# Decoding weight blocks throughout attention, three w_out blocks ahead of the MLP, and softplus as one unit

## The chip, the cores and the metric

The kernel runs on one core of a Trainium2 chip. The metric is the device time of one execution in microseconds (us), the median of several runs. A profile of one further execution tells where the time goes; its span runs from the first to the last recorded instruction.

## The reference

Three stages follow each other; all results are float32.

```
# 1. Nystrom attention, batch 4, heads 8, sequence 576, head size 64, 32 landmarks
A  = softmax(q  @ k_lm.T / 8)      # q_lm, k_lm: means over 18 neighbouring rows
Bm = softmax(q_lm @ k_lm.T / 8)
C  = softmax(q_lm @ k.T / 8)
Z  = Bm.T / (norm1(Bm) * norminf(Bm) + 1e-6);  six times: Z = 2*Z - Z @ Bm @ Z
x  = (A @ Z @ C @ v)               # then (2304 tokens, 512)
# 2. dense MLP, d_ff 2048
h  = x @ w_in;   g = max(h, 0) + log1p(exp(-abs(h)));   x = g @ w_out
# 3. top-1 mixture of 8 experts: token -> argmax(x @ w_gate)
out = gate_prob * sigmoid(x @ w_output_gate)[e] * (relu(x @ w1[e]) @ w2[e])
```

w_in and w_out come as 64-bit floats. The kernel takes them as pairs of 32-bit integers, decodes each block to float32, and splits every matrix operand into a rounded high part and the rest (hi and lo), so that one product is three matmuls: hi*hi, hi*lo and lo*hi.

## The kernel before

**Attention** works on eight groups (a batch and half of its heads). The string PLAN lists its steps: K and V load a group, T transposes it, M makes landmarks, C and A are the two large softmaxes, N the Newton iteration of a batch, E and F the products that end in a batch's x, stored to a DRAM tensor xT_d. W decodes a block of 128 columns of w_in, O a block of 128 rows of w_out, X prepares the first 256 tokens of x. PLAN gives priorities; a planner makes each engine's final order from them, and may bring an instruction forward when its inputs are there and its buffer is free. Attention's q, k and v tiles have three buffers each, and the W, O and X loads use those same buffers from SP's queue. One decode (`decode_f64`, L87) is an Abs on ScalarE (L96) and three integer operations on VectorE (L97, L99, L101); then ScalarE copies the hi part (L106) and GpSimd, in attention, subtracts for the lo part (L107). Ten W blocks (NWA) and one O block are made there.

**The MLP** runs after it in an order written out by hand. Its unit of work is a pair: `gemm1` (L611) makes 256 columns of h for 256 tokens with 24 matmuls, softplus turns them into g, and `gemm2` (L650) adds g's product with two w_out blocks into accumulators with 12 matmuls, two pairs later (LAG). There are 9 chunks of 256 tokens with 8 pairs each; the first three chunks (JOINT) are interleaved, 24 turns, so that each weight block that is decoded serves three chunks. Meanwhile the 21 blocks that attention did not make are loaded by SP (`load_w`, L562) and decoded by VectorE and ScalarE (`weights`, L572), a generator of four units a block. 12 units, three blocks, are taken before the first turn (L876), three and five in the first two turns, and then four a turn, put among the parts of softplus: `softplus_a`, `softplus_b` and `softplus_c` stand at three places of the turn, and the last two belong to the pair before. SP also loads the gate weights (L845) before the second w_out block, and VectorE makes five small tables (L846 to L850) before the loop.

Gating and routing of the tokens are hidden in the later pairs. **The experts** follow, with tiles of 128 tokens; `t_h` (L967) transposes the hidden tile and splits it into hh and hlo, which have three buffers.

Of the kernel before, what the change touches and what calls it, by code (L numbers as in the profile page):

```python
# [1 line left out]

# [27 lines left out]
CH = 256  # L30
# [17 lines left out]
U = 1, 1, 2  # L48
# [38 lines left out]
def decode_f64(nc, pool, src, shape, tag="dect", **kw):  # L87

    w = src.rearrange("p a (n two) -> p a n two", two=2)
    lo32, hi32 = w[:, :, :, 0], w[:, :, :, 1]
    t = pool.tile(shape, I32, tag=tag, name="dect", **kw)
    a = pool.tile(shape, F32, tag="deca", name="deca", **kw)
    nc.scalar.activation(a, hi32.bitcast(F32), AF.Abs, scale=2.0 ** -112)  # L96
    nc.vector.tensor_scalar(t, a.bitcast(I32), 3, None, ALU.logical_shift_left)  # L97
    yield
    nc.vector.scalar_tensor_tensor(t, hi32, -0x80000000, t, ALU.bitwise_and, ALU.bitwise_or)  # L99
    yield  # L100
    nc.vector.scalar_tensor_tensor(a.bitcast(I32), lo32, 29, t, ALU.logical_shift_right, ALU.bitwise_or)  # L101
    yield a
# [13 lines left out]
def moe_nystrom_kernel(ctx: ExitStack, tc: tile.TileContext, q, k, v, w_in, w_out, w_gate, w_ogate, w1, w2,  # L116
# [23 lines left out]
    wo0 = [x0_pool.tile([128, DM], F32R, name=n) for n in ("wo0h", "wo0l")]  # L140


    with ExitStack() as actx:
# [241 lines left out]
        def decode_w_in(i):  # L385
            n = FF // 16
            raw = ld.tile([128, NC6 * 4 * D], I32, tag="kqv"[i % 3], name="raw")
            raw = raw[:, :8 * n].rearrange("p (k f) -> p k f", k=4)
            nc.sync.dma_start(raw, w_in.bitcast(I32).rearrange("(k p) f -> p k f", p=128)[:, :, 2 * n * i:2 * n * (i + 1)])
            a = list(decode_f64(nc, a3, raw, [128, 4, n], bufs=2))[-1]  # L390
            split_hi_lo(nc, a, whi[0][:, :, i * n:(i + 1) * n], wlo[0][:, :, i * n:(i + 1) * n], nc.gpsimd)
# [14 lines left out]
        def prep_x0():  # L406
            xr = ld.tile([128, 4, CH], F32, tag="k", name="x0r")
            nc.sync.dma_start(xr, xT_d[0].rearrange("(k p) n -> p k n", p=128)[:, :, :CH])
            split_hi_lo(nc, xr, x0[0], x0[1], nc.gpsimd)

        def prep_wo0():
            raw = ld.tile([128, 2 * DM], I32, tag="q", name="raw")
            nc.sync.dma_start(raw, w_out.bitcast(I32)[:128, :])
            a = list(decode_f64(nc, a3, raw.unsqueeze(1), [128, 1, DM], bufs=2))[-1]
            split_hi_lo(nc, a[:, 0], wo0[0], wo0[1], nc.gpsimd)
# [12 lines left out]
            "O": lambda _: prep_wo0(),  # L428
# [115 lines left out]
    with ExitStack() as mctx:  # L544
# [27 lines left out]
        def weights():  # L572

            for n, (kind, f) in enumerate(jobs):
                for a in decode_f64(nc, m2, raws.pop(n).unsqueeze(1), [128, 1, DM], tag="x2t"):
                    if a is None:
                        yield
                load_w(n + 3)
                yield
                a = a[:, 0]  # L580
                if kind == "o":
                    split_hi_lo(nc, a, woh[f], wol[f], nc.vector)
                else:
                    split_hi_lo(nc, a.rearrange("p (k f) -> p k f", k=4), wcols(whi, f), wcols(wlo, f), nc.vector)
                yield
# [38 lines left out]
        def softplus_a(h):  # L624
            t = sp.tile([128, 2, CH], F32, tag="t", name="t")
            u = sp.tile([128, 2, CH], F32, tag="u", name="u")
            l = sp.tile([128, 2, CH], F32, tag="l", name="l")
            nc.scalar.activation(t, h, AF.Abs)  # L628
            nc.scalar.activation(t, t, AF.Exp, scale=-1.0)  # L629
            nc.scalar.activation(u, t, AF.Identity, bias=1.0)  # L630
            yield
            nc.scalar.activation(l, t, AF.Ln, bias=1.0)  # L632
            nc.vector.scalar_tensor_tensor(u, u, -1.0, t, ALU.add, ALU.subtract)  # L633
            yield h, u, l

        def softplus_b(h, u, l):

            d = sp.tile([128, 2, CH], F32, tag="d", name="d")
            nc.vector.scalar_tensor_tensor(d, h, 0.0, u, ALU.max, ALU.subtract)  # L639
            nc.vector.tensor_tensor(l, l, d, ALU.add)  # L640
            return l

        def softplus_c(l):
            gh = m3.tile([128, 2, CH], F32R, tag="gh", name="gh")
            gl = m3.tile([128, 2, CH], F32R, tag="gl", name="gl")
# [194 lines left out]
        with tc.manual_schedule():  # L840
# [3 lines left out]
            for nm, src in ((0, w_gate), (1, w_ogate)):  # L844
                nc.sync.dma_start(wg[:, :, nm * NE:(nm + 1) * NE], src.rearrange("(k p) e -> p k e", p=128))  # L845
            nc.vector.tensor_copy(tri_b, cc("tri"))  # L846
            nc.vector.tensor_copy(one_b, cc("ones"))
            nc.vector.memset(osum[:, 0], 0.0)
            nc.vector.tensor_copy(sgn[:, 0], cc("iota")[:1, :NE])
            nc.vector.tensor_scalar(sgn[:, 1], cc("iota")[:1, :NE], -1.0, None, ALU.mult)  # L850
            ga, gs, accs = {}, {}, {}
# [24 lines left out]
            units(12)  # L876
            for i in range(len(order) + LAG):
# [11 lines left out]
                u = ((0, 0, 3), (0, 2, 3))[i] if i < 2 else U  # L889
                if i - 1 in ga:  # L890
                    gs[i - 1] = softplus_b(*ga.pop(i - 1))
                if i < len(order):
# [6 lines left out]
                    units(u[0])  # L899
                    sp_ = softplus_a(h)  # L900
                    next(sp_)
                    if i - 1 in gs:
                        gs[i - 1] = softplus_c(gs[i - 1])
                    ga[i] = next(sp_)
                    units(u[1])
# [4 lines left out]
                if i - 1 in gs and i >= len(order):  # L910
                    gs[i - 1] = softplus_c(gs[i - 1])
                units(u[2])
# [20 lines left out]
    with ExitStack() as ectx:  # L933
# [10 lines left out]

        todo = iter(TAIL)
# [21 lines left out]
        def t_h(hs):  # L967
# [3 lines left out]
            hh = e3.tile([128, 4, 128], F32R, tag="hh", name="hh")  # L971
            hlo = e3.tile([128, 4, 128], F32R, tag="hlo", name="hlo")
# [114 lines left out]
```

## Time and profile before

| | us |
|---|---|
| median of 3 runs (lowest, highest) | 920.24 (918.68, 920.66) |
| the profiled execution's own time | 920.92 |
| its span | 919.1 |
| TensorE busy, share of the span | 863.8, 94% |
| VectorE busy | 660.8, 72% |
| ScalarE busy | 589.2, 64% |
| GpSimd busy | 209.6, 23% |

The profile names TensorE's matmuls PE and its weight loads PEld, VectorE DVE, ScalarE ACT, GpSimd POOL and SyncE SP; an engine's name with a q is its queue of DMA issues. "out<-in" names the tile written and the tiles read, L99 is a line of the kernel, and "xN" after it is a count. An idle time in square brackets stands before the instruction and names what ended it. Attention lies at 0 to 149.3 us of the span, the interleaved pairs at 149.7 to some 290 us, the other pairs reach to 610 us, and the experts to the end.

### The profile page before, as it was taken

Reading aid. Unit: us, or ns where it says so; the run is one execution under the profiler, and the core shown is the slowest. Engines: PE = TensorE matmul, PEld = TensorE weight load, DVE = VectorE, ACT = ScalarE, POOL = GpSimd, SP = SyncE. Lnnn points to the kernel's source line nnn. Section 1 sums busy time; section 2 is a strip of 40 time slices with the busy share of each in tenths; the row PEclk is TensorE's granted clock in tenths of the full one; section 3 lists DMA queues with packets and bytes.
Section 4 is the critical chain, followed back from the end, with each engine's and each line's share of the span. In section 5 each row is a group of like instructions: output and inputs, shape, how many; then the busy total and the mean of one; then the engine's idle time right before and its main releaser. Section 6 shows DMA issues by size and latency. Waiting matters only on the chain.

```text
span 919.1 us, 15441 instructions
## 1 busy us (share of the span) xinstructions
PE 863.8 (94%) x5826; PEld 717.5 (78%) x5826; DVE 660.8 (72%) x1121; ACT 589.2 (64%) x958; POOL 209.6 (23%) x109
## 2 busy tenths in 40 slices
PE   6998987599999999999999999998999999999996
PEld 3665655478788899999999998886878888888885
DVE  0846697787775546665546464668899999999994
ACT  2554564666666655555555555464888888888893
POOL 0001132000000000000000000024666677666662
PEclk9999997799999999999999999999999999999998
DMA  9856466323210000100111000141117459531600
GB/s 228 188 137 182 146 189 194 94 89 92 82 46 13 24 1 24 46 22 4 46 46 47 1 24 1 47 184 47 44 37 264 174 182 378 184 126 34 225 31 33
DMA packets 49516, 90.93 MB, mean 99 GB/s; under 512 B 5471, under 2 KB 32095, under 8 KB 47392
## 3 DMA queue, kind: packets, MB, share of 16 engines
q1 hardware_dynamic: 41408, 74.43, 26.1%
q0 software_dynamic: 3680, 10.78, 3.6%
q10 hardware_dynamic: 4352, 4.72, 1.5%
q8 instruction: 47, 0.77, 0.4%
q14 instruction: 29, 0.24, 0.1%
HBM read 134.46 MB, written 15.48 MB: 163 GB/s over the span
## 4 chain that ended last, share of the span: by engine, by line
PE 68%; DVE 13%; ACT 10%; issue 4%; DMA 4%; POOL 0%; SPq 0%; POOLq 0%; ACTq 0%; DVEq 0%
PE ps_h L618 16%; PE acc L657 14%; PE ps_g L956 12%; PE ps_y L982 11%; DVE dect L99 2%; DVE deca L101 2%; PE ps_hT L970 2%; PE ps_lg L682 2%; ACT t L629 2%; ACT u L630 2%; ACT deca L96 2%; ACT gh L646 1%; DVE u L633 1%; PE ps_t L184 1%; PE ps_t L160 1%
## 5 line engine op out<-in xcount | busy, mean ns | idle before, releaser
L478 DVE TENSOR_TENSOR lo<-raw,hi 128x1024 fp32r<-128x1024 f32 x129 | 228.7, 1799 | 8.8 <-ACT hi L476 8.6
L476 ACT ACTIVATE hi<-raw 128x1024 fp32r<-128x1024 f32 x176 | 176.8, 1063 | 8.4 <-DMA raw<-in_moe_w 8.3
L618 PE MATMUL ps_h<-xh,whi 128*128 128x256 f32 x512 | 147.4, 288 | 5.8 <-DVE d L639 4.1
L618 PE MATMUL ps_h<-xl,whi 128*128 128x256 f32 x512 | 144.9, 283 | 0.3 <-DVE xl L107 0.3
L618 PE MATMUL ps_h<-xh,wlo 128*128 128x256 f32 x512 | 144.8, 283 | 0.0
L647 DVE TENSOR_TENSOR gl<-l,gh 128x512 fp32r<-128x512 f32 x72 | 49.9, 692 | 129.0 <-ACT gh L646 129.0
L485 POOL DMA_INDIRECT xg<-x_d,gidx x23 | 37.8, 1645 | 452.4 <-ACT t L628 441.4
L478 POOL TENSOR_TENSOR lo<-raw,hi 128x1024 fp32r<-128x1024 f32 x47 | 115.9, 2468 | 35.3 <-ACT hi L476 35.2
L618 PEld LDWEIGHTS ps_h<-xh,whi 128*128 128x128 f32 x512 | 98.0, 191 | 11.4 <-DVE d L639 7.9
L618 PEld LDWEIGHTS ps_h<-xl,whi 128*128 128x128 f32 x512 | 98.0, 191 | 1.9 <-DVE xl L107 0.5
L618 PEld LDWEIGHTS ps_h<-xh,wlo 128*128 128x128 f32 x512 | 97.9, 191 | 0.0
L657 PE MATMUL acc<-woh,gh 128*128 128x512 f32 x240 | 96.2, 401 | 0.0
L657 PE MATMUL acc<-wol,gh 128*128 128x512 f32 x240 | 94.5, 394 | 0.0
L657 PE MATMUL acc<-woh,gl 128*128 128x512 f32 x240 | 94.3, 393 | 0.0
L628 ACT ACTIVATE t<-ps_h 128x512 f32<-128x512 f32 x72 | 42.6, 592 | 69.6 <-PE ps_h L618 50.0
L632 ACT ACTIVATE l<-t 128x512 f32<-128x512 f32 x72 | 45.5, 632 | 55.1 <-DVE gl L647 55.1
L982 PE MATMUL ps_y<-hi,hh 128*128 128x512 f32 x184 | 76.7, 417 | 0.2 <-ACT hh L974 0.2
L982 PE MATMUL ps_y<-hi,hlo 128*128 128x512 f32 x184 | 73.3, 398 | 1.7 <-DVE hlo L975 1.6
L956 PE MATMUL ps_g<-hi,x0l 128*128 128x512 f32 x184 | 73.9, 402 | 0.1
L982 PE MATMUL ps_y<-lo,hh 128*128 128x512 f32 x184 | 72.7, 395 | 0.0
L956 PE MATMUL ps_g<-hi,x0h 128*128 128x512 f32 x184 | 72.0, 391 | 0.0
L956 PE MATMUL ps_g<-lo,x0h 128*128 128x512 f32 x184 | 71.9, 391 | 0.0
(263 smaller groups left out, 1790.4 us busy)
## 6 DMA issues: line engine op xcount, KB each, us to landing
raw<-in_moe_w SPq DMA_DIRECT2D x88, 1024.0 KB
raw<-in_moe_w_in SPq DMA_DIRECT2D x16, 512.0 KB
raw<-in_moe_w_out SPq DMA_DIRECT2D x16, 512.0 KB
x_d<-x SPq DMA_DIRECT2D x9, 514.0 KB
k<-in_k SPq DMA_DIRECT2D x8, 576.0 KB
q<-in_q SPq DMA_DIRECT2D x8, 576.0 KB
v<-in_v SPq DMA_DIRECT2D x8, 576.0 KB
xT_d<-xo ACTq DMA_DIRECT2D x16, 288.0 KB
```

Source lines behind the costliest of these rows:

```text
L96: nc.scalar.activation(a, hi32.bitcast(F32), AF.Abs, scale=2.0 ** -112)
L99: nc.vector.scalar_tensor_tensor(t, hi32, -0x80000000, t, ALU.bitwise_and, ALU.bitwise_or)
L476: nc.scalar.activation(w[0][:, us], raw[i][:, us], AF.Copy)
L478: eng.tensor_tensor(w[1][:, us], raw[i][:, us], w[0][:, us].bitcast(F32), ALU.subtract)
L485: nc.gpsimd.indirect_dma_start(out=xg, out_offset=None, in_=src, in_offset=bass.IndirectOffsetOnAxis(ap=gidx[:, s:s + 1], axis=0))
L618: nc.tensor.matmul(ps[:, i], a[:, kk], b_[:, kk], start=n == 0, stop=n == 11)
L628: nc.scalar.activation(t, h, AF.Abs)
L632: nc.scalar.activation(l, t, AF.Ln, bias=1.0)
L647: nc.vector.tensor_tensor(gl, l, gh.bitcast(F32), ALU.subtract)
L657: nc.tensor.matmul(acc[tt], a[:, i, ts_], b_[f], start=f == 0 and n == 0, stop=f == NFF - 1 and n == 2)
L956: nc.tensor.matmul(ps, a[:, kk], b_[:, kk], start=n == 0, stop=n == 11)
L982: nc.tensor.matmul(y, a[:, kk], b_[:, kk], start=half == 0 and n == 0, stop=half == 1 and n == 11)
```

## The change

The decoding steps get buffers of their own (tag raw, two buffers) and their loads are issued from GpSimd's queue. Attention makes eight W blocks and three O blocks instead of ten and one; they are spread over PLAN, from after E1 on. The MLP takes no units before the loop. One softplus function does the whole of a pair's softplus in its own turn and takes three units at fixed places, none in turn 0; `EXTRA` adds one unit in turn 0 and three more in turns 5 and 8. A block's decode is begun with the split of the block before it. The number of blocks decoded in the loop is 21 as before. The gate's loads and the small tables move from before the loop to turn 2. The pools psm and pss change places in PSUM, and hh and hlo of the experts lie in the w_out tiles that attention filled.

```diff
-K1 T0 M0 M1 A0 C0 T1 K2 M2 C1 K3 V0 A1 K4 V1 T2 E0 C2 E1 T3 M3 N0 V2 K5 K6 V3 T4 A2 C3 A3 F0 V4 E2 M4 A4 M5 T5 K7 E3
-N1 X0 V5 M6 C4 T6 C5 C6 E4 M7 V6 V7 N2 A5 E5 W0 F1 N3 W1 W2 E6 W3 T7 A6 W4 O0 C7 A7 W5 F2 W6 E7 W7 F3 W8 W9
+K1 T0 M0 M1 A0 C0 T1 K2 M2 C1 K3 V0 A1 K4 V1 T2 E0 C2 E1 W0 T3 M3 N0 W1 V2 K5 K6 V3 T4 W2 A2 C3 A3 F0 W3 V4 E2 M4 A4
+W4 M5 T5 K7 E3 W5 N1 X0 V5 M6 C4 W6 T6 C5 C6 E4 M7 V6 V7 N2 A5 W7 E5 F1 N3 O0 E6 T7 A6 C7 A7 O1 F2 E7 O2 F3
-NWA = 10
+NWA = 8
+NWO = 3
+EXTRA = 0, 5, 8
...
     nc.scalar.activation(a, hi32.bitcast(F32), AF.Abs, scale=2.0 ** -112)
+    yield
     nc.vector.tensor_scalar(t, a.bitcast(I32), 3, None, ALU.logical_shift_left)
-    yield
     nc.vector.scalar_tensor_tensor(t, hi32, -0x80000000, t, ALU.bitwise_and, ALU.bitwise_or)
-    yield
     nc.vector.scalar_tensor_tensor(a.bitcast(I32), lo32, 29, t, ALU.logical_shift_right, ALU.bitwise_or)
     yield a
...
+        psm = actx.enter_context(tc.tile_pool(name="psm", bufs=1, space=PSUM))
         pss = actx.enter_context(tc.tile_pool(name="pss", bufs=2, space=PSUM))
-        psm = actx.enter_context(tc.tile_pool(name="psm", bufs=1, space=PSUM))
...
-            raw = ld.tile([128, NC6 * 4 * D], I32, tag="kqv"[i % 3], name="raw")
-            raw = raw[:, :8 * n].rearrange("p (k f) -> p k f", k=4)
-            nc.sync.dma_start(raw, w_in.bitcast(I32)...)
+            raw = ld.tile([128, 8 * n], I32, tag="raw", name="raw", bufs=2).rearrange("p (k f) -> p k f", k=4)
+            nc.gpsimd.dma_start(raw, w_in.bitcast(I32)...)
...
-        def prep_wo0():
-            raw = ld.tile([128, 2 * DM], I32, tag="q", name="raw")
-            nc.sync.dma_start(raw, w_out.bitcast(I32)[:128, :])
+        def prep_wo(f):
+            raw = ld.tile([128, 2 * DM], I32, tag="raw", name="raw", bufs=2)
+            nc.gpsimd.dma_start(raw, w_out.bitcast(I32)[f * 128:(f + 1) * 128, :])
...
         def weights():
+            dec = {}
+            def start(n):
+                if n < len(jobs):
+                    dec[n] = decode_f64(nc, m2, raws.pop(n).unsqueeze(1), [128, 1, DM], tag="x2t")
+                    next(dec[n])
+            def finish(n):
+                if n < len(jobs):
+                    dec[n] = next(dec[n])[:, 0]
+                    load_w(n + 3)
+            start(0)
+            finish(0)
+            yield
             for n, (kind, f) in enumerate(jobs):
...
+                nc.scalar.activation(hi, a, AF.Copy)
+                start(n + 1)
                 yield
+                nc.vector.tensor_tensor(lo, a, hi.bitcast(F32), ALU.subtract)
+                yield
+                finish(n + 1)
                 yield
...
+        def softplus(h, units):
...
             nc.scalar.activation(t, h, AF.Abs)
             nc.scalar.activation(t, t, AF.Exp, scale=-1.0)
             nc.scalar.activation(u, t, AF.Identity, bias=1.0)
             nc.scalar.activation(l, t, AF.Ln, bias=1.0)
+            units(1)
             nc.vector.scalar_tensor_tensor(u, u, -1.0, t, ALU.add, ALU.subtract)
             nc.vector.scalar_tensor_tensor(d, h, 0.0, u, ALU.max, ALU.subtract)
             nc.vector.tensor_tensor(l, l, d, ALU.add)
             nc.scalar.activation(gh, l, AF.Copy)
+            units(1)
             nc.vector.tensor_tensor(gl, l, gh.bitcast(F32), ALU.subtract)
+            units(1)
             return gh, gl
...
-            units(12)
             for i in range(len(order) + LAG):
...
                     h = gemm1(p, xs[c], *HB.get(i, ()))
...
+                    gs[i] = softplus(h, units if i else int)
+                    if i in EXTRA:
+                        units(1 if i == 0 else 3)
+                    if i == 2:
+                        nc.vector.tensor_copy(tri_b, cc("tri"))
...
+        hht = cycle([[wo0[j][f].rearrange("p (k n) -> p k n", k=4) for j in range(2)] for f in range(NWO)])
...
-            hh = e3.tile([128, 4, 128], F32R, tag="hh", name="hh")
-            hlo = e3.tile([128, 4, 128], F32R, tag="hlo", name="hlo")
+            hh, hlo = next(hht)
```

## Rows read from the trace of the kernel before

**Rows 1.** The page: busy time by engine, then TensorE and DMA in 40 slices.
```profile
PE 863.8 (94%) x5826; PEld 717.5 (78%) x5826; DVE 660.8 (72%) x1121; ACT 589.2 (64%) x958; POOL 209.6 (23%) x109
...
PE   6998987599999999999999999998999999999996
...
DMA  9856466323210000100111000141117459531600
```
**Rows 2.** Windows: from:to, length, busy us (instructions) by engine, TensorE clock, DMA share, GB/s.
```profile
9.84:149.67 139.83, 126.45 (x1580) 81.22 (x1580) 95.64 (x267) 75.79 (x171) 16.95 (x12) 0.97 0.68 178
5.00:35.00 30.00, 23.89 (x293) 15.97 (x294) 12.70 (x41) 11.94 (x31) 0.00 (x0) 1.00 1.10 247
120.00:149.67 29.67, 22.89 (x186) 12.38 (x185) 28.35 (x59) 18.76 (x38) 10.11 (x8) 0.88 0.60 182
149.67:176.63 26.96, 15.59 (x85) 14.18 (x86) 17.83 (x29) 13.71 (x24) 0.24 (x1) 0.69 0.44 141
176.63:277.31 100.68, 94.86 (x578) 80.81 (x576) 79.67 (x131) 66.42 (x114) 0.00 (x0) 1.00 0.25 76
```
**Rows 3.** TensorE in order of time: start, duration, line, tiles, count, idle before.
```profile
9.84 1.19 PE L184 MATMUL ps_t<-cst,k 96*128 96x96 f32 x6 [6.48 <-DMA cst<-in_consts]
...
92.71 0.69 PE L204 MATMUL ps_lm<-lmc,l 128*64 128x64 f32 x16 [2.94 <-ACT l L200]
...
147.97 1.33 PE L377 MATMUL ps_x<-at,wbd 64*128 64x288 f32 x4
149.67 0.58 PE L618 MATMUL ps_h<-x0h,whi 128*128 128x256 f32 x1 [0.37 <-ACT xo L379]
...
171.34 0.79 PE L657 MATMUL acc<-wo0h,gh 128*128 128x512 f32 x1 [11.37 <-ACT gh L646]
...
176.63 0.35 PE L618 MATMUL ps_h<-xh,whi 128*128 128x256 f32 x1
```
**Rows 4.** The chain that ended last, in order of time: start, duration, what.
```profile
151.56 6.49 DMA raw<-in_moe_w_out
...
280.45 2.75 PE acc L657 x12
283.20 2.87 PE ps_h L618 x24
```
**Rows 5.** VectorE and ScalarE in one turn of the interleaved pairs.
```profile
186.16 0.68 DVE L633 SCALAR_TENSOR_TENSOR u<-u,t 128x512 f32<-128x512 f32 x1
186.76 0.69 DVE L99 SCALAR_TENSOR_TENSOR dect<-raw,dect 128x512 int32<-128x512 int32 x1
187.48 0.69 DVE L101 SCALAR_TENSOR_TENSOR deca<-raw,dect 128x512 int32<-128x512 int32 x1
...
189.32 0.58 ACT L628 ACTIVATE t<-ps_h 128x512 f32<-128x512 f32 x1
...
191.13 0.62 ACT L646 ACTIVATE gh<-l 128x512 fp32r<-128x512 f32 x1
```
**Rows 6.** VectorE in order of time: two A steps, each first and last instruction.
```profile
42.68 0.78 DVE L320 STREAM_TRANSPOSE asm<-ps_a 128x576 f32<-128x576 f32 x1 [0.71 <-PE ps_a L218]
...
48.02 0.78 DVE L331 STREAM_TRANSPOSE at<-asm 128x576 f32<-128x576 f32 x1
...
132.33 0.71 DVE L320 STREAM_TRANSPOSE asm<-ps_a 128x576 f32<-128x576 f32 x1
...
145.34 0.77 DVE L331 STREAM_TRANSPOSE at<-asm 128x576 f32<-128x576 f32 x1
```
**Rows 7.** VectorE's groups at 120 to 149.67 us: line, shapes, count, busy, mean ns.
```profile
L99 DVE SCALAR_TENSOR_TENSOR dect<-raw,dect 128x512 int32<-128x512 int32 x7 | 7.0, 1005 | 0.0
...
L97 DVE TENSOR_SCALAR dect<-deca 128x512 int32<-128x512 int32 x7 | 3.5, 498 | 0.8 <-ACT deca L96 0.8
```
**Rows 8.** SP's issues: start, time until the last is issued, line, tiles, count.
```profile
5.26 6.84 SPq L173 DMA_DIRECT2D v<-in_v  x3
```
**Rows 9.** ScalarE in order of time: a decode that waits for its load.
```profile
91.16 1.22 ACT L96 ACTIVATE deca<-raw 128x512 f32<-128x512 f32 x2 [3.05 <-DMA raw<-in_moe_w_in]
```

More of the change, by code (lines that the diff above doesn't have):

```diff
@@ L1 @@
 from contextlib import ExitStack, nullcontext
+from itertools import cycle
 import numpy as np
@@ L47 @@
 LEAD = 1
-U = 1, 1, 2
 LAG = 2
@@ L139, in moe_nystrom_kernel @@
     x0 = [x0_pool.tile([128, 4, CH], F32R, name=n) for n in ("x0h", "x0l")]
-    wo0 = [x0_pool.tile([128, DM], F32R, name=n) for n in ("wo0h", "wo0l")]
+    wo0 = [[x0_pool.tile([128, DM], F32R, name=f"{n}{f}") for f in range(NWO)] for n in ("woh", "wol")]
     with ExitStack() as actx:
@@ L427, in moe_nystrom_kernel @@
             "X": lambda _: prep_x0(),
-            "O": lambda _: prep_wo0(),
+            "O": prep_wo,
             "W": decode_w_in,
@@ L553, in moe_nystrom_kernel @@
         pa = pool("pa", 1, space=PSUM)
-        woh = [wo0[0]] + [wo.tile([128, DM], F32R, name=f"woh{f}") for f in range(1, NFF)]
-        wol = [wo0[1]] + [wo.tile([128, DM], F32R, name=f"wol{f}") for f in range(1, NFF)]
-        due = [(3 * (f // 2) + 2 * (f == 1), "o", f) for f in range(1, NFF)]
+        woh = wo0[0] + [wo.tile([128, DM], F32R, name=f"woh{f}") for f in range(NWO, NFF)]
+        wol = wo0[1] + [wo.tile([128, DM], F32R, name=f"wol{f}") for f in range(NWO, NFF)]
+        due = [(3 * (f // 2) + 2 * (f == 1), "o", f) for f in range(NWO, NFF)]
         due += [(3 * (f // 2) - 2, "i", f) for f in range(NWA, NFF)]
@@ L572, in weights @@
         def weights():
-            for n, (kind, f) in enumerate(jobs):
[L575 to L578, printed above, removed]
-                yield
[L580 to L584, printed above, removed]
+            dec = {}
[10 more added lines that the diff above has]
+            yield
+            for n, (kind, f) in enumerate(jobs):
+                if kind == "o":
+                    a, hi, lo = dec.pop(n), woh[f], wol[f]
+                else:
+                    a, hi, lo = dec.pop(n).rearrange("p (k f) -> p k f", k=4), wcols(whi, f), wcols(wlo, f)
+                nc.scalar.activation(hi, a, AF.Copy)
+                start(n + 1)
+                yield
+                nc.vector.tensor_tensor(lo, a, hi.bitcast(F32), ALU.subtract)
+                yield
+                finish(n + 1)
                 yield
@@ L843, in moe_nystrom_kernel @@
             load_w(0)
[L844 to L851, printed above, removed]
+            gs, accs = {}, {}
             side = iter(())
@@ L898, in moe_nystrom_kernel @@
                         next(side, None)
[L899 to L905, printed above, removed]
+                    gs[i] = softplus(h, units if i else int)
[3 more added lines that the diff above has]
+                        nc.vector.tensor_copy(tri_b, cc("tri"))
+                        nc.vector.tensor_copy(one_b, cc("ones"))
+                        nc.vector.memset(osum[:, 0], 0.0)
+                        nc.vector.tensor_copy(sgn[:, 0], cc("iota")[:1, :NE])
+                        nc.vector.tensor_scalar(sgn[:, 1], cc("iota")[:1, :NE], -1.0, None, ALU.mult)
+                        for nm, src in ((0, w_gate), (1, w_ogate)):
+                            nc.sync.dma_start(wg[:, :, nm * NE:(nm + 1) * NE], src.rearrange("(k p) e -> p k e", p=128))
                     if i == nj - 1:
@@ L909, in moe_nystrom_kernel @@
                         xs[c + 1] = split_x(load_xr(c + 1))
-                if i - 1 in gs and i >= len(order):
-                    gs[i - 1] = softplus_c(gs[i - 1])
-                units(u[2])
                 if i >= len(order):
```

23 lines of the change are left out of this document (7 added, 16 removed).

## The prediction

> **What bounds the kernel now.** I read the page first: TensorE is busy for 94% of the span, so time can only come from where it idles or runs slowly, and the slices show that at the front, in the first, fifth to eighth and last of 40 [rows 1]. The windows then split that front into stages [rows 2]. In attention TensorE is busy 126.45 of 139.83 us at a mean clock of 0.97; VectorE is loose on the whole (95.64 us) but full at its end, 28.35 of 29.67 us. From the first MLP matmul to the fourth pair, 26.96 us, TensorE works 15.59 us at a clock of 0.69. In the interleaved turns after that it works 94.86 of 100.68 us. TensorE's order of time tells what the middle window waits for [rows 3]: attention's last matmul ends at 147.97 + 1.33 = 149.30 us, the first gemm1 starts at 149.67, and after three of them the first gemm2 idles 11.37 us for ScalarE's gh. The chain of waits shows what stands ahead of that gh, a 6.49 us load of a w_out block, and also what a pair costs where TensorE alone is the limit: 2.87 us for 24 matmuls of gemm1 and 2.75 us for 12 of gemm2, 5.62 us [rows 4]. After turn 18 this is the pace, and nothing of the change touches it.
>
> **The change part by part.** The sum is made against the profiled execution, 920.92 us (span 919.1 and 1.82 around it), 0.68 us above the median shown.
>
> *The wait before the first gemm2.* 12 units, three whole blocks, stand ahead of the first softplus and go; the w_out blocks 0 to 2 come from attention, so gemm2 of the first two pairs lacks none but block 3, which is decoded in turns 0 and 1. What is late next is the first softplus itself. Its chain by the distances of the same operations in a turn [rows 5]: from t to the fourth ScalarE operation 191.13 - 189.32 = 1.81 us; u ends some 0.1 us after that, then three VectorE operations in a row at 0.72 us each (187.48 - 186.76), a gh of 0.62, a gl of 0.69: 5.5 us. Two more gemm1 take 2 x 2.87 = 5.74 us meanwhile, so the stall goes to about nothing; that cover is gone if the splitting of x, which sits ahead on both engines, ends over 0.2 us late. So 11.37 us go. The 12 matmuls of the first gemm2 took 176.63 - 171.34 = 5.29 us after this idle time; at full pace 2.75, so 2.54 more go. The first three gemm1 took 171.34 - 11.37 - 149.67 = 10.30 us instead of 8.61, because TensorE was on its low clock after the thin end of attention; that 1.69 us I leave in. Sum -13.9 us; ends -15.6 (those too) and -10.9 (a stall of 3 us for a late gl).
>
> *The interleaved turns.* 16 turns (3 to 18) take 100.68 us [rows 2], 6.29 each against 5.62: 10.8 us are lost, and neither VectorE (79.67) nor ScalarE (66.42) is full, so it is their waiting for each other in the written order. The new order of one turn on VectorE, with 0.60 us between independent and 0.72 between dependent operations [rows 5]: u, d, l at 0.72, 0.72, then gh on ScalarE (0.7) and gl 1.4 us after l starts, with lo in between; 0.6 for gl, 0.45, 0.72 and 0.6 for the three decode operations: 5.2 us. ScalarE has t, exp, u, ln, hi, the next Abs and gh, and is free for the next t 4.7 us after this one. Behind gh, which waits for l, stands the next pair's t, and that has till 5.62. So the turn fits under TensorE, with 0.39 us to spare. The turns 5 and 8 take a second block, whose hi, lo and three decode operations follow each other in some 3.3 us. Two of them, 6.6 us, less 0.39 x 8 and a start margin of 0.3, leave a stall of about 3.2 us. So -10.8 + 3.2 = -7.6; ends -10.8 (lag hides both) and -4 (every turn 0.22 longer as well). The later pairs use the same softplus without units: 2.76 us of VectorE in 5.62, hidden.
>
> *Attention, its end.* The last A step runs on VectorE from 132.33 to 146.11 us, and an early one from 42.68 to 48.80, 6.1 us against 13.8 [rows 6]. Between its operations stand seven decodes, whose three operations are 7.0, 4.7 and 3.5 us [rows 7]. With those gone earlier, up to 7.7 us go from the end, since the last ps_x wait for that step.
>
> *Attention, its start.* The planner issues loads when a buffer is free, not where PLAN has them: SP issues V0, V1 and V2 by 12 us [rows 8]. GpSimd's queue is empty, so I expect W0 and W1, 1.05 MB, in the first microseconds, beside the loads on which the first transpose waits until 9.84 us [rows 3]. In that stretch the DMA engines are full, 247 GB/s [rows 2], so the two blocks push back the rest by 1.05/0.247 = 4.25 us at most, by nothing if SP's queue is served first. I take the 4.25, as full engines leave no spare. The Trainium skill, DMA: Bandwidth & Descriptors, section SWDGE vs HWDGE vs iDMA, says that loads from GpSimd and from SP lie in different queues of each DMA engine, which serves them in turn. By it the early blocks do get their share and the sum has the 4.25, without it 0; no row here shows both queues in that stretch.
>
> *Attention, loads that come late.* One decode waits 3.05 us for its block on ScalarE [rows 9], with the copies of another group behind it, and TensorE idles 2.94 us [rows 3]. I keep one such wait. With 11 early blocks in full DMA queues there may be more: the bound is 11 x 2.94 = 32 us, the other end is none. I take the row nearest, one as before, since SP's loads no longer share buffers with the blocks. GpSimd's 11 lo operations stay, and its issues stand between them. The Trainium skill, SBUF — State Buffer, section SBUF: two separate sides, speaks against the move: while VectorE holds the port that it shares with GpSimd, GpSimd can't write the descriptors of its loads. Here L99 takes 1.005 us beside GpSimd's subtractions [rows 7] against 0.69 in a turn [rows 5], so the two do meet; by that rule a load could lose an operation like L97, 0.5 us, and all 11 would be 5.5 us, most of it hidden by the second buffer.
>
> Attention: -7.7 + 4.25 = -3.5 us. Its floor: all idle time, 139.83 - 126.45 = 13.4, and 3% of clock, 4.2, go: -17.6.
>
> Sum: -3.5 - 13.9 - 7.6 = -25.0, 895.9 us in the profiled run, about 895 as a median.
>
> **Rivals.**
> 1. *Blocks land late and stretch attention.* Four loads of the kind of [rows 9] in the full stretch: 4 x 2.94 - 3.5 = +8.3 us in attention, total -13.2: 907. For it: the planner doesn't know how full the queues are. Against: after 40 us they are far from full [rows 1].
> 2. *Attention becomes as dense as TensorE allows*: -17.6 + 4.25 = -13.4, total -34.9: 886. For it: its VectorE has 44 us free. Against: Newton and A steps are chains.
> 3. *x comes late.* If the tiles of x lie where attention's last tiles were, their load starts at its end: 6.49 and some 1.6 us of splitting, against 3.3 until the second gemm1, +4.8: 900. Against: nothing of their pool changes.
> 4. *The decodes don't spread*, because GpSimd's queue holds loads behind lo operations that wait for ScalarE: no change in attention, 899.
> 5. *Slower: the fused softplus doesn't fit a turn.* ScalarE's gh waits for VectorE's l in the same turn and holds up hi, the next Abs and the next t. It turns the total to a loss when a turn passes 6.29 + 17.4/16 = 7.4 us; at 7.6 it is 16 x 1.31 = +21, total 924. For it: the turn today takes 6.29 with both engines a fifth idle. Against: the 5.2 us above, from measured distances.
>
> **How the numbers follow.** Forecast 0.46, rivals 0.22, 0.14, 0.07, 0.05 and 0.06. The time is the forecast's, 895. The range 883 to 910 takes in rivals 1 to 4 for the most part; outside lie rival 5 and the far tails of 1 and 2, together under 0.2. A measurement of this kernel can't tell less than 0.2%, 1.8 us, from no change. Slower 0.07: rival 5 and the far end of rival 1's 32 us. Same 0.03, faster 0.90.
>
> **What would show it.** In the trace after: no idle time of over 2 us before the first gemm2, and its 12 matmuls near 2.75 us; 16 turns in 90 to 94 us, with TensorE idle only near turns 6 and 9; two block loads on GpSimd's queue before 5 us and the first transpose near 14 us; the last A step in 6 to 8 us and attention's end near 146. I am wrong if ScalarE's Abs waits for raw again and again, if the first transpose isn't later, or if a turn stays at 6.2 us.

## The result, and the profile after

The changed kernel takes 925.01 us (median of 5 runs, 924.38 to 925.52) against 919.72 for the kernel before beside it: 1.0058 times, 95% interval 1.0044 to 1.0071. It is slower by 0.6%, and the forecast of 895 is wrong in sign. The page of the profile after hardly differs in TensorE's busy time [rows 1], while the span is 4.1 us longer, so on balance the loss is idle time. In the slices TensorE is thinnest in the first two, and its granted clock dips in the second, fifth and eighth.

```profile
PE 863.9 (94%) x5826; PEld 722.4 (78%) x5826; DVE 662.5 (72%) x1121; ACT 586.3 (64%) x958; POOL 218.8 (24%) x121
...
PE   4698899889998999999999998998999999999996
...
PEclk9899899999999999999999999999999999999999
DMA  9947424433210000100111000141107459531600
```

Both traces are cut at the same four instructions (gemm1 of turn 3, gemm1 of turn 19, a gemm1 at the end of the pairs, the last instruction), so that each row can be set beside a term of the forecast's sum.

| stretch | before | after | difference | forecast |
|---|---|---|---|---|
| to turn 3 | 176.63 | 172.40 | -4.2 | -3.5 - 13.9 = -17.4 |
| turns 3 to 18 | 100.68 | 97.05 | -3.6 | -7.6 |
| pairs after that | 321.27 | 332.20 | +10.9 | 0 |
| the rest, mostly experts | 320.52 | 321.55 | +1.0 | 0 |
| span | 919.1 | 923.2 | +4.1 | -25.0 |

The windows that give these lengths follow: first two of the kernel before that [rows 2] does not have, then those of the kernel after, the last two with the slow clock that two places below speak of. After the length stand busy us (instructions) of TensorE, its weight loads, VectorE, ScalarE and GpSimd, then TensorE's granted clock, the DMA share and GB/s.

```profile
277.31:598.58 321.27, 317.18 (x2097) 288.50 (x2098) 176.56 (x424) 182.50 (x322) 2.07 (x2) 1.00 0.08 25
598.58:919.10 320.52, 307.84 (x1486) 252.33 (x1484) 290.56 (x273) 249.51 (x327) 190.11 (x91) 0.99 0.39 139
```

```profile
163.70:172.40 8.70, 6.26 (x37) 5.22 (x38) 5.84 (x11) 6.87 (x13) 0.00 (x0) 1.00 0.71 216
172.40:269.45 97.05, 92.18 (x578) 83.30 (x576) 89.25 (x148) 71.25 (x123) 0.00 (x0) 0.98 0.32 99
269.45:601.65 332.20, 322.01 (x2098) 292.35 (x2097) 185.71 (x429) 181.85 (x324) 2.00 (x2) 0.98 0.08 25
601.65:923.20 321.55, 308.13 (x1486) 252.27 (x1484) 283.27 (x272) 249.01 (x326) 191.23 (x91) 0.99 0.39 139
40.00:45.00 5.00, 2.88 (x22) 1.95 (x22) 3.48 (x10) 2.80 (x7) 0.00 (x0) 0.50 0.65 179
444.00:449.00 5.00, 5.00 (x19) 4.04 (x19) 2.94 (x5) 2.33 (x4) 0.00 (x0) 0.66 0.00 0
```

TensorE in order of time (start, duration, line, tiles, idle before) says how the first stretch lost what it had won. The 11.37 us before the first gemm2 [rows 3] are 1.44, near the nothing that was forecast. But the first transpose is 3.2 us later than before, and two idle times of 5.63 and 3.58 us are new; attention's last matmul, ps_x, ends at 163.70 instead of 149.30. (Two of the MLP's first three gemm1, 5.74 us at full pace, now run ahead of it, so not all of these 14.4 us are lost.)

```profile
13.00 1.20 PE L185 MATMUL ps_t<-cst,k 96*128 96x96 f32 x6 [9.64 <-DMA cst<-in_consts]
...
42.12 0.59 PE L161 MATMUL ps_c<-dense 128*128 128x512 bf16 x1 [5.63 <-ACT ec L310]
...
93.29 0.59 PE L161 MATMUL ps_t<-dense 128*128 128x512 bf16 x1 [3.58 <-ACT lm L208]
...
162.94 0.76 PE L378 MATMUL ps_x<-at,wbd 64*128 64x288 f32 x4
164.69 0.38 PE L634 MATMUL ps_h<-xh,whi 128*128 128x256 f32 x1 [1.00 <-ACT xo L380]
...
169.27 0.50 PE L669 MATMUL acc<-woh,gh 128*128 128x512 f32 x1 [1.44 <-ACT gh L656]
```

ScalarE in the same stretch shows what stands behind them: the Abs of the first two blocks that it finds late, and the copy of x0r.

```profile
9.92 0.66 ACT L98 ACTIVATE deca<-raw 128x512 f32<-128x512 f32 x1 [7.89 <-DMA raw<-in_moe_w_in]
...
40.69 0.66 ACT L98 ACTIVATE deca<-raw 128x512 f32<-128x512 f32 x1 [6.17 <-DMA raw<-in_moe_w_in]
...
91.91 1.06 ACT L107 ACTIVATE x0h<-x0r 128x1024 fp32r<-128x1024 f32 x1 [6.50 <-DMA x0r<-xT_d]
```

and GpSimd's issues say why the one at 40.69 is late: two loads go at 1.31, but the fifth, which needs the buffer of the third, goes only at 30.19, after that one's decode, and arrives 10.5 us later.

```profile
1.31 1.73 POOL L389 DMA_DIRECT2D raw<-in_moe_w_in  x2 [0.86 <-POOLq L1076]
13.04 0.75 POOL L389 DMA_DIRECT2D raw<-in_moe_w_in  x1 [9.99 <-DVE deca L102]
...
18.75 0.77 POOL L389 DMA_DIRECT2D raw<-in_moe_w_in  x1 [3.58 <-ACT qT L187]
...
30.19 0.76 POOL L389 DMA_DIRECT2D raw<-in_moe_w_in  x1 [9.36 <-DVE dect L100]
```

The planner did not spread the decodes as PLAN has them: with free buffers of their own it put six of the eight W blocks into the first 45 us. (With the same PLAN and the old shared buffers, in e10 below, three blocks are begun in the first 55 us, the earliest at 39.19.)

In the pairs after turn 19 TensorE was busy for 317.18 of 321.27 us before. Now its idle time there grows from 4.09 to 10.19 us, in a few places where it waits for copies of ScalarE's, and its busy time grows by 4.83 us, at a mean granted clock of 0.98 instead of 1.00. So of the +10.9 some 6 us are waits and the rest are matmuls that ran slower. ScalarE in one such turn, before a chunk's first use of a new x:

```profile
295.06 0.60 ACT L648 ACTIVATE t<-ps_h 128x512 f32<-128x512 f32 x1 [0.57 <-PE ps_h L634]
...
296.89 0.61 ACT L651 ACTIVATE l<-t 128x512 f32<-128x512 f32 x1
299.34 0.63 ACT L656 ACTIVATE gh<-l 128x512 fp32r<-128x512 f32 x1 [1.83 <-DVE l L655]
299.87 0.61 ACT L107 ACTIVATE xh<-xr 128x512 fp32r<-128x512 f32 x1
```

Its gh stands 1.83 us idle for VectorE's l, in the same turn, with the copy xh queued behind it. TensorE pays at 300.54, with 2.83 us for that xh against 1.75 at the same copy before. The largest new idle time, at 443.46, has a load in it too: x2t stood behind copies xh that had waited 1.52 us for their xr.

```profile
300.54 0.38 PE L634 MATMUL ps_h<-xh,whi 128*128 128x256 f32 x1 [2.83 <-ACT xh L107]
...
443.46 1.07 PE L694 MATMUL ps_lg<-wg,x2t 128*128 128x16 f32 x8 [2.17 <-ACT x2t L689]
```

```profile
441.78 1.15 ACT L107 ACTIVATE xh<-xr 128x512 fp32r<-128x512 f32 x2 [1.52 <-DMA xr<-xT_d]
```

### The profile page after: what moved, and what is told of

The parts are those of the page before. It is cut to its first block, busy times and chain, and to the rows that moved or that the text cites. A ratio compares the mean times of both kernels' runs of the same rounds, so it can differ in the third digit from the quotient of the medians.

```text
span 923.2 us, 15425 instructions
## 1 busy us (share of the span) xinstructions
PE 863.9 (94%) x5826; PEld 722.4 (78%) x5826; DVE 662.5 (72%) x1121; ACT 586.3 (64%) x958; POOL 218.8 (24%) x121
## 4 chain that ended last, share of the span: by engine, by line
PE 66%; DVE 13%; DMA 8%; ACT 6%; issue 5%; POOL 1%; SPq 0%; POOLq 0%; DVEq 0%; ACTq 0%
PE ps_h L634 19%; PE acc L669 15%; PE ps_g L959 9%; PE ps_y L984 8%; DMA raw<-in_moe_w 3%; DVE lo L478 2%; ACT hi L476 2%; DMA raw<-in_moe_w_in 2%; PE ps_lg L694 2%; PE ps_hT L973 1%; PE ps_t L185 1%; DVE dect L101 1%; PE ps_u L290 1%; DMA cst<-in_consts 1%; DVE l L655 1%
## 5 line engine op out<-in xcount | busy, mean ns | idle before, releaser
L478 DVE TENSOR_TENSOR lo<-raw,hi 128x1024 fp32r<-128x1024 f32 x129 | 222.1, 1748 | 15.5 <-ACT hi L476 15.3
L476 ACT ACTIVATE hi<-raw 128x1024 fp32r<-128x1024 f32 x176 | 177.0, 1063 | 11.7 <-DMA raw<-in_moe_w 11.4
L656 ACT ACTIVATE gh<-l 128x512 fp32r<-128x512 f32 x72 | 45.5, 632 | 115.3 <-DVE l L655 115.3
L653 DVE SCALAR_TENSOR_TENSOR u<-u,t 128x512 f32<-128x512 f32 x72 | 49.6, 689 | 84.9 <-ACT u L650 84.9
L669 PE MATMUL acc<-woh,gh 128*128 128x512 f32 x256 | 103.5, 404 | 1.4 <-ACT gh L656 1.4
L669 PE MATMUL acc<-wol,gh 128*128 128x512 f32 x256 | 101.3, 396 | 0.0
L669 PE MATMUL acc<-woh,gl 128*128 128x512 f32 x256 | 101.0, 395 | 0.0
L634 PEld LDWEIGHTS ps_h<-xh,wlo 128*128 128x128 f32 x512 | 99.8, 195 | 0.0
L984 PE MATMUL ps_y<-hi,woh 128*128 128x512 f32 x184 | 76.5, 416 | 0.0
L984 PE MATMUL ps_y<-hi,wol 128*128 128x512 f32 x184 | 73.5, 399 | 1.1 <-DVE wol L977 1.1
L984 PE MATMUL ps_y<-lo,woh 128*128 128x512 f32 x184 | 72.6, 395 | 0.0
```

The source lines that it names most:

```text
L476: nc.scalar.activation(w[0][:, us], raw[i][:, us], AF.Copy)
L478: eng.tensor_tensor(w[1][:, us], raw[i][:, us], w[0][:, us].bitcast(F32), ALU.subtract)
L634: nc.tensor.matmul(ps[:, i], a[:, kk], b_[:, kk], start=n == 0, stop=n == 11)
L669: nc.tensor.matmul(acc[tt], a[:, i, ts_], b_[f], start=f == 0 and n == 0, stop=f == NFF - 1 and n == 2)
L984: nc.tensor.matmul(y, a[:, kk], b_[:, kk], start=half == 0 and n == 0, stop=half == 1 and n == 11)
```

## Experiments

Ratios are to the kernel before, run beside each on the same chip (918.79 to 919.32 us), with 95% intervals.

| kernel | us | ratio |
|---|---|---|
| e1_sp_queue | 925.57 | 1.0061 (1.0043 to 1.0079) |
| e2_hold | 931.86 | 1.0135 (1.0115 to 1.0155) |
| e3_late3 | 914.84 | 0.9961 (0.9947 to 0.9975) |
| e4_attn_before | 911.16 | 0.9916 (0.9896 to 0.9937) |
| e5_attn_late3 | 901.56 | 0.9815 (0.9792 to 0.9837) |
| e6_hold_pool | 933.01 | 1.0160 (1.0132 to 1.0188) |
| e7_best_spread | 906.58 | 0.9857 (0.9831 to 0.9884) |
| e8_no_swap | 911.44 | 0.9920 (0.9899 to 0.9942) |
| e9_plan_old | 919.47 | 1.0007 (0.9988 to 1.0026) |
| e10_bufs_old | 919.95 | 1.0009 (0.9994 to 1.0024) |
| e11_spread_late3 | 911.81 | 0.9938 (0.9918 to 0.9959) |
| e12_plan_old_3bufs | 915.37 | 0.9958 (0.9944 to 0.9972) |
| e13_bufs3 | 916.18 | 0.9970 (0.9958 to 0.9982) |
| e14_best3 | 905.17 | 0.9861 (0.9840 to 0.9881) |

### The later pairs: softplus in three parts (e3_late3)

```diff
-                    gs[i] = softplus(h, units if i else int)
+                    if i < SW:                              # SW = 20
+                        gs[i] = softplus(h, units if i else int)
+                    else:                                   # t, exp, u | gh of the pair before | l, VectorE's u
+                        sp_ = softplus_a(h); next(sp_)
+                        if i > SW: gs[i - 1] = softplus_c(gs[i - 1])
+                        ga[i] = next(sp_)
...
```

> The changed kernel with softplus in the three parts of before from turn 20 on, when no block is left to decode; turns 0 to 19 stay fused. Theory B (in the fused order ScalarE's gh waits 1.8 us for VectorE's l, and the splits of x, the transposes' copies and the gate behind it come late): the 10.9 us that the turns after 19 lose against the kernel before return, 8 to 11 us of it, total 914 to 917, and TensorE's waits of 2.8, 2.2 and 1.8 us at 300, 443 and 584 us go. Rival (those waits come from something else, as the moved gate loads or the memory layout): total 922 to 926.

Measured 914.84, 10.2 us below the changed kernel, as the theory of the later pairs had it. Between the same two gemm1 the pairs take 322.83 us instead of 332.20, so 9.4 of the 10.9 us are back there; TensorE's three waits are not all gone, but as in the kernel before (1.75 us for xh). The other runs with the fused form take 329.4 to 332.6 us there, those with three parts 321.3 to 323.0. The same turn of ScalarE now has gh, of the pair before, without a wait, and t waits 1.78 us for TensorE instead of 0.57: that difference is the slack that xh, x2t and the copies of x use up.

```profile
290.00 0.63 ACT L669 ACTIVATE u<-t 128x512 f32<-128x512 f32 x1
290.54 0.61 ACT L684 ACTIVATE gh<-l 128x512 fp32r<-128x512 f32 x1
291.91 0.63 ACT L671 ACTIVATE l<-t 128x512 f32<-128x512 f32 x1 [0.76 <-DVE gl L685]
294.33 0.60 ACT L667 ACTIVATE t<-ps_h 128x512 f32<-128x512 f32 x1 [1.78 <-PE ps_h L635]
```

### Attention: the old decodes (e4_attn_before), and the queue (e1_sp_queue)

```diff
-(PLAN after)   nc.gpsimd.dma_start(raw, ...)   tag="raw", bufs=2
+(PLAN before, W8 W9 made O1 O2)   nc.sync.dma_start(raw, ...)   tag="kqv"[i % 3]      # e4
+(PLAN after)                      nc.sync.dma_start(raw, ...)   tag="raw", bufs=2     # e1
```

> The changed kernel with the attention stage of before: its PLAN (W8 and W9 replaced by O1 and O2), loads on SP's queue into the q, k and v buffers; MLP and PSUM order of the change stay. Theory A: attention ends near 149 us, turn 3 starts near 163 instead of 172.4, total 914 to 918. Rival (the early decodes pay for themselves, the loss lies all in the MLP): total 922 to 930.

> The changed kernel (925.0 us) with the decoding loads of attention on SP's queue instead of GpSimd's, still with their two buffers. Theory A (the early decodes wait for loads in full DMA queues, whoever issues them): ScalarE still waits over 5 us for a block before 50 us, attention ends within 4 us of 163.7, total 921 to 929. Rival (loads from GpSimd's queue are slow or jump the line in themselves): the first transpose is back near 9.8 us, no wait over 3 us for raw, attention ends near 150, total about 912 to 916.

e4 took 911.16, 13.9 us below the changed kernel and a little under what was expected; its turn 3 starts at 160.83 against 172.40. So the decodes in attention cost 11.6 of the 13.9 us ahead of turn 3. e1 took 925.57: which queue issues the loads makes no measurable difference to the time. Its first transpose starts at 10.99 instead of 13.00 us, but its ScalarE waits for blocks and x0r are 26.1 us.

### Holding the loads back (e2_hold, e6_hold_pool)

```diff
+        holds = [ld.tile([128, 1024], I32, tag="raw", name="hold", bufs=2) for _ in range(2)]
...
+        for j, t in enumerate(holds):       # just ahead of W0
+            nc.vector.tensor_tensor(junk[:TP, j:j + 1], t[:TP, :1].bitcast(F32), R[3]["k"][:, 0, :1], ALU.add)   # e2
+            nc.gpsimd.tensor_tensor(...)                                                                         # e6
```

> The changed kernel with its two decoding buffers held back until group 3's k has landed (a small VectorE addition that reads both), so that no block is loaded in the first 35 us; GpSimd's queue, PLAN and all else stay. Theory A: the first transpose starts near 9.8 us (3.2 us earlier), the 6.2 us wait of ScalarE near 40 us is gone with its slow clock (8 us), so attention ends 8 to 13 us earlier and the total is 913 to 918. Rival (the decodes themselves, not when they are loaded, stretch attention): attention ends within 4 us of 163.7, total 921 to 929.

> The changed kernel, with both raw buffers held by a small GpSimd add that reads group 3's k, so that the first block loads are issued some 30 us later and no engine but GpSimd waits for it. Theory A (the blocks loaded in the first 30 us push back the loads that attention needs, and their decodes hold ScalarE's queue up): the first transpose of a k is back near 9.8 us, no decode waits over 3 us before 45 us, and of the 13.9 us that the old attention gives back 4 to 8 come: 917 to 921. Rival C (eleven decodes with two buffers and loads from this queue wait wherever they stand): the early loss goes and comes back between 45 and 140 us; 923 to 927.

Both missed, 931.86 and 933.01, slower than any range given for them. The first transpose went back (9.72 and 9.75 us), but a late load was not a late decode. In e2 VectorE itself stood 8.61 us for k at 33.03. In e6 only GpSimd waited, and yet ScalarE had the Abs where the planner had put it, ahead of the copies of the next group, and stood there for 11.16 us:

```profile
38.74 0.66 ACT L98 ACTIVATE deca<-raw 128x512 f32<-128x512 f32 x1 [11.16 <-DMA raw<-in_moe_w_in]
```

Meant to relieve attention, this run shows the price instead: a load that is late at an Abs stops all that stands behind it on ScalarE, in its written order.

### Places, buffers, and a third buffer (e9_plan_old, e10_bufs_old, e12_plan_old_3bufs, e13_bufs3)

```diff
-PLAN after;  tag="raw", bufs=2;  GpSimd's queue
+PLAN before; tag="raw", bufs=2;  GpSimd's queue      # e9
+PLAN after;  tag="kqv"[i % 3];   SP's queue          # e10
+PLAN before; tag="raw", bufs=3;  GpSimd's queue      # e12, dect with one buffer to make room
+PLAN after;  tag="raw", bufs=3;  GpSimd's queue      # e13, dect with one buffer to make room
```

> The changed kernel with the old places of the decodes in PLAN (W and O after N2, E5 and later; O1 and O2 for the last two W), but with its two raw buffers and its loads from GpSimd's queue kept. x0r then is the first to use a raw buffer and needs xT_d, so no block is decoded in attention's first half. Theory F (what costs attention its time is where the decodes stand, in the full first 40 us, not the buffers or the queue): the first transpose of a k is back near 9.8 us and the time within 3 us of the kernel with the old attention, 909 to 914. Rival G (the two buffers and GpSimd's queue cost by themselves): 919 to 925.

> The other half: the new places of the decodes in PLAN, but in the q, k and v buffers and loaded by SP, as before. The shared buffers keep a block's load from being issued ahead of the k, q and v that stand before it in PLAN, so that the first decode comes at about 40 us. Theory F: no decode before 35 us, the first transpose near 9.8 us, and 909 to 916. Rival H (decodes among the Newton and A steps of the first half lengthen them wherever they stand): attention stays some 10 us longer than with the old places, 920 to 925.

> As the kernel with the old places in PLAN, its own raw buffers and GpSimd's loads (919.5), but with three raw buffers instead of two (a decode's temporary on VectorE has one buffer instead of two, to make room). There x0r holds one of the two buffers from the start, and ScalarE waits 18.7 us in all for blocks and x0r. Theory I (attention pays for ScalarE's in-order wait at the Abs of a block whose load is not in, since copies of other groups stand behind it): an earlier issue cuts these waits to under 9 us and the time to 911 to 915. Rival J (the decodes themselves, or GpSimd's queue, take the time): 918 to 921.

> The changed kernel (925.0) with three raw buffers instead of two, its new places in PLAN kept. Theory I with the full DMA engines of the first 40 us as the reason for the late blocks: three blocks now go out in the first microseconds, the first transpose of a k is later than 13 us, and the time is 923 to 929. Rival K (only the lack of a third buffer makes the blocks late): ScalarE's waits fall under 12 us, and 914 to 919.

e9 and e10 each gave back some 5 us (919.47, 919.95): theory F missed, and the rivals' ranges, which they touch, leave the other 5 to 9 us to be explained. Neither the places nor the buffers do it alone. (The profiled executions were 921.99 and 914.83 us, so that of e10 is 5.1 below its median.) What most of the runs go with is ScalarE's time at an Abs or at x0h for a load that is not in. The waits of ScalarE up to 165 us (waited for: us in total, times, longest), first of the changed kernel, then of e9, e12 and e13:

```profile
ACT deca L98 <- DMA raw<-in_moe_w_in: 15.5, 5, 7.9
...
ACT x0h L107 <- DMA x0r<-xT_d: 6.5, 1, 6.5
...
ACT deca L98 <- DMA raw<-in_moe_w_out: 2.5, 2, 2.1
```

```profile
ACT deca L98 <- DMA raw<-in_moe_w_in: 7.4, 5, 2.7
...
ACT x0h L107 <- DMA x0r<-xT_d: 5.8, 1, 5.8
ACT deca L98 <- DMA raw<-in_moe_w_out: 5.5, 1, 5.5
```

```profile
ACT x0h L107 <- DMA x0r<-xT_d: 5.8, 1, 5.8
...
ACT deca L98 <- DMA raw<-in_moe_w_in: 3.7, 2, 2.4
```

```profile
ACT deca L98 <- DMA raw<-in_moe_w_in: 9.4, 3, 8.2
...
ACT x0h L107 <- DMA x0r<-xT_d: 6.2, 1, 6.2
...
ACT deca L98 <- DMA raw<-in_moe_w_out: 1.8, 1, 1.8
```

| | after | e9 | e13 | e10 | e12 | e4 |
|---|---|---|---|---|---|---|
| ScalarE's waits for blocks and x0r, us | 24.5 | 18.7 | 17.4 | 15.2 | 9.5 | 4.9 |
| of these at the first Abs, before any transpose | 7.9 | 0 | 8.2 | 0 | 0 | 0 |
| first transpose at | 13.00 | 9.78 | 12.77 | 9.64 | 9.97 | 9.89 |
| first gemm2 starts at | 169.27 | 166.98 | 162.73 | 165.38 | 160.94 | 157.71 |

The wait at the first Abs held up nothing by itself, for ScalarE's next copies for attention had to wait for the first transpose, which waited for the constants. Without it, and counted from the first transpose to the first gemm2, the runs stand in one order: waits of 4.9, 9.2, 9.5, 15.2, 16.6 and 18.7 us go with 147.8, 150.0, 151.0, 155.7, 156.3 and 157.2 us, some 0.7 us for each us of wait (an estimate from the two ends). e1 is in line with its 26.1 and 161.4 us; of the runs below with softplus in three parts, e11 is some 1 us out with its 14.2 and 156.7. The two runs that hold loads back are not: e2 has 17.0 and 166.1 us, with VectorE's own wait of 8.61 us, and e6 27.6 and 168.9 us.

The third buffer is the direct test, as it leaves PLAN and queue alone; the planner's order moves with it. In e12 it takes the waits from 18.7 to 9.5 and the first gemm2 6.0 us forward; the time of 915.37 lies just outside the theory's 911 to 915 and well below the rival's 918. In e13 it takes 8.8 us off the changed kernel, where I had expected full DMA engines to keep it at 923 or more: that part of my theory fell. Rival K's time held, and of its waits under 12 us only this much, that 17.4 are 9.2 without the first Abs. The wait of 6.17 us at 40.69 is gone, since the load of that fifth block now goes at 18.51 instead of 30.19, and its Abs finds it:

```profile
29.80 0.69 ACT L98 ACTIVATE deca<-raw 128x512 f32<-128x512 f32 x1
```

What e13 keeps is what three buffers can't help: blocks loaded beside the first k, q and constants, with the first transpose at 12.77 us, and 6.2 us for x0r.

### The first gemm2, the PSUM pools and the turns (e8_no_swap, e7_best_spread)

```diff
-psm, pss (after)                               # e8: e4 with the pools in the order of before
+pss, psm
-EXTRA = 0, 5, 8;  units(1 if i == 0 else 3)    # e7: e5 with the same units in other turns
+EXTRA = 0, 3, 4, 5, 6, 7, 8;  units(1)
```

> The kernel with the old attention's decodes (911.16), but with the PSUM pools in the order of the kernel before, so that the MLP's first gemm1 can't start until attention's last tiles are read. Theory E (two gemm1 run inside attention's last 10 us only because of the exchange of the pools): three gemm1 stand behind attention's end again, 2 x 2.87 us and a second half of clock recovery, 4 to 7 us slower: 915 to 918. Rival (the wait for x and for the first gh absorbs it): 911 to 913.

> As the kernel with both repairs, but the six extra units of turns 5 and 8 are given one each to turns 3 to 8. Theory D (a turn with three extra units doesn't fit under TensorE, one with a single one nearly does): the idle times of 2.4 and 0.7 us for VectorE's d and the slow turns behind them go, 3 to 5 us below the kernel with both repairs, about 897. Rival (six turns each pass 5.62 by the length of one unit, some 0.6 us): the same time as with both repairs, within 1 us.

e8 took 911.44, the same as e4: the rival held. The exchange let two gemm1 run in attention's tail in e4, but there TensorE then idles 3.51 us for xo, and the first gemm2 starts at 157.71 in the one, 157.68 in the other. e8 also has the MLP's start in one piece, as before, and so measures two terms of the sum by themselves:

```profile
147.40:160.43 13.03, 13.03 (x85) 12.54 (x86) 8.05 (x13) 8.56 (x16) 0.23 (x1) 0.86 0.39 129
160.43:255.82 95.39, 92.18 (x577) 83.31 (x576) 87.66 (x145) 69.47 (x121) 0.00 (x0) 0.98 0.32 100
```

The three gemm1 and the first gemm2 take 13.03 us with TensorE always busy, against 26.96 [rows 2]: -13.93, the forecast's -13.9. Turns 3 to 18 take 95.39: -5.3. Every other run with these turns, e3 among them, takes 95.4 to 95.6 there, so 1.5 of the changed kernel's 97.05 us are found in no other trace.

e7 is 5 us slower than e5, so its theory fell, and its rival of no change with it, and ScalarE shows why. A unit that starts with the hi copy stands right behind the three VectorE operations which make its input; the next turn's t is behind it. In the changed kernel that is the turn with three extra units; ScalarE, and then TensorE:

```profile
195.80 0.63 ACT L656 ACTIVATE gh<-l 128x512 fp32r<-128x512 f32 x1 [1.00 <-DVE l L655]
198.99 0.63 ACT L595 ACTIVATE whi<-deca 128x512 fp32r<-128x512 f32 x1 [2.55 <-DVE deca L102]
...
200.09 0.57 ACT L648 ACTIVATE t<-ps_h 128x512 f32<-128x512 f32 x1
```

```profile
203.59 0.39 PE L634 MATMUL ps_h<-xh,whi 128*128 128x256 f32 x1 [2.44 <-DVE d L654]
```

One extra unit has the same first copy, so e7 pays it in more turns, among them this one:

```profile
172.69 0.64 ACT L658 ACTIVATE gh<-l 128x512 fp32r<-128x512 f32 x1 [1.42 <-DVE l L657]
175.88 0.63 ACT L597 ACTIVATE woh<-deca 128x512 fp32r<-128x512 f32 x1 [2.55 <-DVE deca L103]
...
176.97 0.58 ACT L650 ACTIVATE t<-ps_h 128x512 f32<-128x512 f32 x1
```

and its turn 5 takes 9.16 us instead of e5's 6.02.

### Versions that beat both (e5_attn_late3, e11_spread_late3, e14_best3)

e5 is e4 and e3 together, e11 is e10 and e3, e14 is e12 and e3; their diffs are those above.

> The two repairs in one kernel: attention with the old PLAN places and loads of the decodes (eight W and three O blocks, the last two W made O1 and O2), and the old softplus in three parts from turn 20 on. Theory (two separate losses, one in attention and one in the later pairs): the gains of the two single repairs add, 925.0 - 13.9 - 10.2 = 901, within 2 us. Rival (both repairs uncover the same later wait): less than the sum, 905 to 911.

> The one before, with softplus in three parts from turn 20 on as well. Theory (the two losses are separate, as the sum of the two single repairs showed): 10.2 us below the one before. Rival: less than 7 us below it.

> The first of these with softplus in three parts from turn 20 on. Theory (separate losses): 10 us below the first of these, 901 to 905 if theory I holds there. Rival: less than 7 us below it.

e5 took 901.56, against the 901 of the two gains added; e11 and e14 lie 8.1 and 10.2 us below e10 and e12, so the rival of under 7 us fell both times. The two losses are separate, within 2 us. e5 is the best of all, 0.9815 (0.9792 to 0.9837) of the kernel before: the change's MLP front, with the old decodes in attention and the old softplus where no blocks are decoded.

## Why the prediction was wrong

**The first gemm2: right.** Forecast -13.9, and e8 has -13.93, term by term: no stall, 10.28 us for the first three gemm1 (10.30 left in) and 2.75 for the first gemm2.

**Attention: wrong, and the largest part of the miss.** The sum had -3.5. With the -13.9 taken out of the -4.2 up to turn 3, attention has +9.7. Its term for the start was about right in size (the first transpose is 3.2 us later, forecast 4.25). Two steps failed. "I keep one such wait" at 2.94 us: ScalarE waits 24.5 us for blocks and x0r, in eight places (16.6 without the first Abs), and TensorE idles 5.63 and 3.58 us behind two of them. The sentence beside it, that SP's loads no longer share buffers with the blocks, had the sign wrong: the old shared buffers were what kept the planner from decoding early, and two buffers of one's own mean that a block's load can't go before the decode two places ahead is done. And the -7.7 for the last A step did not reach attention's end: that step runs from 147.00 to 152.44 + 0.78 us, 6.2 us as forecast, but it begins at 147.00 instead of 132.33. Rival 1 named this mechanism, and its +8.3 us for attention came near the +9.7. That is in part luck, as it had four equal waits of 2.94 us, and all of the -7.7 on the other side. What it took as its reason, blocks that land late in full engines, is half of it: the load that ScalarE waited for until 40.69 did take 10.5 us in full engines, but it also went 11.7 us later than with a third buffer (30.19 against 18.51 in e13), and with that the wait was gone. The prediction's own sign of being wrong, an Abs that waits for raw again and again, is the one that came.

**The interleaved turns: right in kind, too large.** Of the -10.8 for turns at 5.62 us, all came: 16 x 5.62 is 89.9, and the turns away from the extra units take 5.62. The stall of the turns with extra units was forecast at 3.2 us and costs 95.39 - 89.9 = 5.5 in e8, 7.1 in the changed kernel. TensorE's idle time in e8 is 95.39 - 92.18 = 3.2 us, the forecast's size; the other 2.3 us are matmuls that ran slower, at a mean granted clock of 0.98, and the sum had that at nothing. That the idle time fits is in part luck: I counted it as a chain of VectorE's operations in such a turn, and not what ScalarE's queue adds, the hi copy that stands 2.55 us idle behind three of them with the next t behind it.

**The later pairs: wrong.** The step was "2.76 us of VectorE in 5.62, hidden". Hidden on VectorE it is; but ScalarE, in order, waits at gh for l in 52 places, 93.3 us in all (1.83, with 0.57 us to spare, in the turn shown), and so has no room left for xh, x2t and x. That is +10.9 us, some 6 of idle time and 5 of slower matmuls at a clock of 0.98, and e3 gives 9.4 of them back in that stage. Rival 5 had exactly this wait; it looked for its price in the interleaved turns, where no x is split and 5.62 us held. So the sign it gave came true by its mechanism in another place, and its 0.06 was too low because I asked only whether a turn fits, not what else shares the queue. That its total of 924 lies so near the measured 925.01 is luck: it had attention 3.5 us faster.

**A slip in the reading.** The prediction has the kernel before thin in the fifth slice; that digit is a 9, and the thin ones are the sixth to eighth [rows 1]. Nothing was worked out from it.

**Two rules weighed.** The Trainium skill, DMA: Bandwidth & Descriptors, section SWDGE vs HWDGE vs iDMA, has the queues of GpSimd and SP served in turn. The trace agrees: the first transpose, which waits for the constants on SP's queue, comes 3.2 us later beside two blocks on GpSimd's, and 1.2 us later in e1, where SP's queue has all loads. The Trainium skill, SBUF — State Buffer, section SBUF: two separate sides, has GpSimd's descriptor writes held up while VectorE holds the port that they share. No cost of it shows in the time, for e1, without those writes, takes 925.57 us.

**What stays open.** How the waits turn into time is shown by the third buffer and by the order of seven runs; why e2 and e6 lie off that order was not tried. The fused softplus in the interleaved turns came together with a new order of the decodes, and no run parts the two. The part after 601.65 us is 1.0 us longer; the other runs take 319.6 to 322.4 us there, so this may be no more than one execution's difference from another.

## What to carry to other kernels

An engine that runs in order pays for each wait with everything that stands behind it, as ScalarE's 6.17 us at 40.69 became 5.63 of TensorE's: before a step is called hidden, list what is queued behind its waiting instruction, not only how long the engines are busy. Giving a stream of loads two buffers of its own does two things at once, as it lets a planner start early and makes the load after next wait for a release; count releases against load time before the loads are moved. A fused form of a step that does no harm in one loop can be wrong in the next, where other work shares its engine (9.4 us here), and it pays to choose by loop.

## What the hardware showed that was not expected

The granted clock can fall behind short idle times too. Around the 5.63 us without work that ended at 42.12 it was at its low level (0.50, 1.2 GHz) from 40 to 45 us, and after the 2.17 us that ended at 443.46 it was 0.66 on average from 444 to 449 us, so that a turn of 7.32 us in the kernel before became 10.97, with idle time for only 2.17 of the 3.65 us. Not each such time has a fall behind it: after the 2.44 us that ended at 203.59 it was 1.00 to 209 us, and in the window of the 1.44 us before the first gemm2 it was 1.00 as well: its 12 matmuls took 3.13 us, against 5.29 after the 11.37 us of before. A block's load from GpSimd's queue took 10.5 us from its issue until ScalarE had it, with the DMA share at 1.08 from 30 to 41 us; one of the same size from SP's took 6.49 in the kernel before [rows 4], with the share at 0.89. The two were not tried at the same load, so this is no comparison of the queues.
